# A pre-LN attention and GEGLU block: VectorE's exponential in one product of 2048 columns, 84 of 512 quads on VectorE, 12 slots turned there, and a new order

## The chip, the core and the metric

One Trainium2 chip, one of its cores, one launch. The metric is the device time of the kernel in microseconds (us); smaller is better. Beside the times there is one execution recorded by the hardware profiler. Engines are called as the profile calls them: PE is the matmul engine and PEld its weight load, ACT is ScalarE, DVE is VectorE, POOL is GpSimd, and SP issues the DMAs.

## What is computed

The input `x` has 2048 rows of 640 bf16 numbers. With `ln` for a layer norm without gain and bias:

```
qkv = ln(x) @ wqkv                       # 32 heads of 20
p   = softmax(q @ k.T * 20**-0.5)        # per head, 2048 x 2048
h   = x + concat(p @ v) @ wo
out = h + (gelu_tanh(ln(h) @ w_gate) * (ln(h) @ w_up)) @ w_down     # 640 -> 1728 -> 640
```

The exponentials are 32 x 2048 x 2048 numbers, 134 million; on 128 partitions these are 2048 tiles of 128 x 512.

## The kernel before

**Tiles and quads.** Scores are made transposed: 128 keys on the partitions, queries in the columns. Heads go in groups of four (`g`, 8 of them), which use four row groups of PE. A tile is 128 x 512 scores of one head, and the four tiles of one group over the same keys are a quad: 512 quads in all. The queries are taken in chunks (`QR`): first 512 queries for the first six groups, then chunks of 256, and at the end four of 128. A chunk is cut into slots, 33 in all, most of them of 16 quads; slot 31 has 12 and slot 32 has 4.

**Two ways to an exponential.** Most tiles go through ACT: a unit of two or three PSUM banks is filled by score matmuls (`unit`, line 1154; matmuls, L1175) and read by one ACTIVATE of 1024 or 1536 columns. Two sets of banks alternate, (0,1,2) and (3,4), so that PE fills one while ACT reads the other; in the slots of `FOUR` they are (0,1) and (2,3), so every instruction there has 1024 columns. The tiles of `D_QUADS[slot]` quads go to DVE instead (`d_exp`, line 1104). For each of the four tiles, a TENSOR_SCALAR of 512 columns (L1116) takes the scores out of PSUM as int16 numbers whose high bits are the exponent and whose low seven are the fraction. After the fourth, 2048 columns are worked at once: one TENSOR_SCALAR cuts out the fraction (`y`), a TENSOR_TENSOR multiplies it by the raw value, in `D_SPLIT` pieces (lines 1123 to 1126), and a second TENSOR_SCALAR reduces the raw value to its power of two (`v`). Both `y` and `v` are multiplied with the values by PE, so that each quad on DVE costs PE twice the attention-times-values work. These helpers record all instructions as L560.

**Where a DVE tile's scores lie.** In a slot of `DIN`, a DVE tile that falls due at a unit of three banks takes the third bank of that set; ACT then reads only two. This is called an inset here. The bank comes free when DVE has taken the tile out. In the other slots, and in all slots of `FOUR`, the tile has a background bank (7, 5 or 4) of its own. `D_LEAD` says by how many ACT tiles a DVE tile is placed ahead.

**Epilogue of a slot** (`epilogue`, line 1266). The sum of a slot collects in bank 6. For the chunks in `TURN`, DVE turns it by a 32 x 32 transpose, divides, turns it back, and four DMAs per slot write it to HBM, from where one DMA per chunk gathers it. For other chunks DVE copies it out, PE transposes it in four fp32 blocks (L1302), and DVE divides; from the third chunk on SP then issues a DMA transpose for each 128 rows.

**Background.** The projections of later groups and chunks, the output projection, layer norm and MLP of finished chunks (L866, L1417, L1537, their evacuations on DVE, tanh on ACT) run between all this.

**Order.** Nothing is ordered by the hardware. `Sched` lists some 6,700 operations with a cost and a priority and plans a start for each; every engine's program is the order that comes out. `NUDGE` adds to the sort key of single operations, and `HOLD` keeps an operation back until another has been started. An engine executes in that order, and waits on semaphores where the operation at its head isn't ready. The first 29 us are a prologue (load `x`, layer norm, transposes, keys and queries of the first group). The end is a tail: output projection, layer norm, MLP of the last 128 rows after the last exponential.

Of the kernel before, what the change touches and what calls it, by code (L numbers as in the profile page):

```python
# [47 lines left out]
class Sched:  # L48
# [325 lines left out]
FOUR = (24, 25)  # L374
DIN = (6, 14, 17, 18, 20, 23, 24, 27, 29, 30, 31, 32)
# [22 lines left out]
TURN = (3, 4, 6, 7, 8)  # L398
# [8 lines left out]
D_SPLIT = 2  # L407
D_LAG = 2
D_QUADS = (0, 0, 3, 2, 3, 3, 3, 3, 3, 2, 3, 3, 3, 1, 3, 3, 4, 2, 4, 3, 3, 3, 4, 3, 3, 3, 2, 2, 4, 3, 1, 2, 1)
D_FIRST, D_PART = 2, 0.8  # L410
D_LEAD = ((0, 0, 0, 0, 0, 0, 0, 0), (0, 21, 15, 8, 38, 7, 13, 18, 19, 16, 22, 21, 14, 33, 19, 19, 14, 7, 8, 10, 20, 0, 27, 25, 15))
# [127 lines left out]
def bass_sequential_preLN__mha_block__glu_gated_geglu__prompt_kernel(  # L539
# [12 lines left out]
    with ExitStack() as es:  # L552
# [709 lines left out]
        def epilogue(s_, bk, d_sums):  # L1262
# [7 lines left out]
            tb = rbase(c)  # L1270
            if c in TURN:
                n = len(gs)
# [378 lines left out]
```

## Time and profile before

| | us |
|---|---|
| runs | 854.5, 855.43, 855.63 |
| median | 855.43 |
| profiled execution | 855.09 |
| its span, first to last instruction | 853.3 |

In the profile, a group of instructions has a line, an engine, an operation, what it writes and reads, and a count; behind these come its busy time, the mean duration of one, and the idle time of the engine just before them with what ended it. Durations of ACT and DVE overlap a little: the next instruction starts before the last one's recorded end. What one instruction costs in a row of them is therefore read from the chain of work or from starts, not from the mean.

### The profile page before, as it was taken

The page shows a single profiled execution, that of the slowest core. Times are in us where ns is not written, and L with a number is a line of the kernel's source. Part 1 is how long each engine was busy: PE and PEld are TensorE (multiplying, and loading weights), DVE is VectorE, ACT ScalarE, POOL GpSimd, SP SyncE. Part 2 cuts the span into 40 slices and gives each one's busy share as a digit, 9 for nine tenths or more (in the row PEclk, how much of TensorE's full clock was granted, in tenths as well). Part 3 has the DMA queues.
Part 4 walks back from the last instruction along what each step waited for, and adds up shares of the span by engine and source line. Part 5 has one row for each costly group of instructions (what it writes and reads, how often), then busy time and mean ns, then how long its engine had stood idle before and what let it go on. Part 6 is the DMA issues. An engine that isn't in the chain of part 4 may idle for free.

```text
span 853.3 us, 31794 instructions
## 1 busy us (share of the span) xinstructions
PE 810.5 (95%) x14355; PEld 418.2 (49%) x14381; DVE 736.1 (86%) x1451; ACT 828.8 (97%) x824; POOL 65.2 (8%) x194
## 2 busy tenths in 40 slices
PE   8999999999999999999989999998999999999998
PEld 4433232233345554554444445444455666667677
DVE  8735888989989989978999899989998898897884
ACT  7999999999999999999999999999999999999992
POOL 6600000000101000100001000010002020020100
PEclk9999999999999999999999999999999999999999
DMA  8211113632431001001000100011001110101000
GB/s 277 83 34 52 44 36 78 166 84 69 133 95 20 7 14 32 18 19 36 7 21 2 26 25 2 18 28 30 7 22 14 45 21 16 38 4 27 11 12 17
DMA packets 41943, 36.07 MB, mean 42 GB/s; under 512 B 17524, under 2 KB 39968, under 8 KB 41808
## 3 DMA queue, kind: packets, MB, share of 16 engines
q1 hardware_dynamic: 41808, 34.04, 15.0%
q8 instruction: 113, 1.85, 1.0%
q14 instruction: 22, 0.18, 0.1%
HBM read 21.51 MB, written 9.40 MB: 36 GB/s over the span
## 4 chain that ended last, share of the span: by engine, by line
ACT 84%; PE 10%; DVE 3%; DMA 1%; POOL 1%; issue 1%; SPq 0%
ACT pts L560 55%; ACT rege L560 27%; ACT qt_all L560 3%; PE ps L1175 2%; PE ps L1537 2%; PE ps L560 2%; PE ps L1417 1%; PE ps L866 1%; DMA rege<-in_A_x_dram 1%; DVE qt_all L1116 1%; DVE rege L1116 0%; DVE rege L560 0%; PE ps L800 0%; DVE stats L560 0%; PE ps L861 0%
## 5 line engine op out<-in xcount | busy, mean ns | idle before, releaser
L560 ACT ACTIVATE pts<-ps 128x1536 bf16<-128x1536 f32 (+1 forms) x483 | 553.0, 1321 | 0.5 <-PE ps L1175 0.4
L1175 PE MATMUL ps<-qt_all,kt_all 32*128 32x256 bf16 (+2 forms) x4736 | 317.8, 257 | 25.9 <-ACT pts L560 8.2
L560 ACT ACTIVATE rege<-ps 128x1536 bf16<-128x1536 f32 (+1 forms) x235 | 281.8, 1319 | 0.6 <-PE ps L1175 0.5
L1175 PEld LDWEIGHTS ps<-qt_all,kt_all 32*128 32x128 bf16 x4736 | 118.9, 92 | 217.7 <-ACT pts L560 91.8
L1116 DVE TENSOR_SCALAR qt_all<-ps 128x512 int16<-128x512 f32 x176 | 118.7, 681 | 15.3 <-PE ps L1175 14.4
L1417 PE MATMUL ps<-rege,regw 128*128 128x256 bf16 (+1 forms) x1128 | 128.2, 250 | 1.5 <-DVE qt_all L1116 0.8
L1116 DVE TENSOR_SCALAR rege<-ps 128x512 int16<-128x512 f32 x160 | 108.1, 683 | 15.1 <-PE ps L1175 14.5
L560 PE MATMUL ps<-pts,v_all 128*21 128x256 bf16 (+2 forms) x2648 | 118.5, 260 | 0.7 <-ACT pts L560 0.6
L1417 PEld LDWEIGHTS ps<-rege,regw 128*128 128x128 bf16 x1128 | 81.1, 98 | 35.9 <-issue 18.2
L560 PE MATMUL ps<-rege,v_all 128*21 128x256 bf16 (+2 forms) x1676 | 97.0, 267 | 0.4 <-DVE rege L560 0.2
L866 PE MATMUL ps<-regw 128*128 128x512 bf16 (+1 forms) x283 | 67.8, 343 | 3.3 <-issue 1.7
L1537 PE MATMUL ps<-regw,rege 128*128 128x320 bf16 x378 | 69.7, 302 | 0.6 <-DVE rege L1376 0.3
L560 PEld LDWEIGHTS ps<-pts,v_all 128*21 128x21 bf16 x2648 | 57.2, 91 | 26.2 <-issue 18.2
L560 DVE TENSOR_SCALAR qt_all<-qt_all 128x2048 int16<-128x2048 int16 (+3 forms) x118 | 58.0, 496 | 0.9
L560 PEld LDWEIGHTS ps<-rege,v_all 128*21 128x21 bf16 x1676 | 41.4, 91 | 23.9 <-issue 16.8
L560 POOL CAST mv<-mv 128x4 bf16<-128x4 f32 (+2 forms) x13 | 3.6, 274 | 543.3 <-DVE mv L560 543.2
L1537 PEld LDWEIGHTS ps<-regw,rege 128*128 128x128 bf16 x378 | 30.1, 97 | 24.0 <-issue 9.7
L1462 DVE TENSOR_SCALAR rege<-ps 128x512 bf16<-128x512 f32 (+2 forms) x54 | 35.1, 653 | 5.7 <-PE ps L1417 4.8
L866 PEld LDWEIGHTS ps<-regw 128*128 128x128 bf16 x303 | 23.6, 97 | 32.4 <-issue 16.9
L1476 DVE SCALAR_TENSOR_TENSOR qt_all<-qt_all,ps 128x512 bf16<-128x512 f16 (+2 forms) x54 | 35.0, 649 | 4.3 <-PE ps L1417 2.8
L560 ACT ACTIVATE qt_all<-qt_all 128x512 f16<-128x512 f16 (+2 forms) x54 | 38.3, 739 | 0.0
L560 DVE TENSOR_SCALAR rege<-rege 128x2048 int16<-128x2048 int16 x54 | 37.0, 685 | 0.7
(150 smaller groups left out, 826.7 us busy)
## 6 DMA issues: line engine op xcount, KB each, us to landing
q_rows<-regw SPq DMA_DIRECT2D x20, 128.0 KB, 1.8
out_dram<-rege SPq DMA_DIRECT2D x16, 160.0 KB, 1.8
regw<-in_A_wqkv_dram SPq DMA_DIRECT2D x3, 800.0 KB, 11.1
rege<-in_A_x_dram SPq DMA_DIRECT2D x7, 320.0 KB, 4.0
regw<-in_B_w_gate_dram SPq DMA_DIRECT2D x5, 432.0 KB, 3.4
regw<-in_B_w_up_dram SPq DMA_DIRECT2D x5, 432.0 KB, 3.3
rege<-in_A_x_dram SPq DMA_DIRECT2D x3, 640.0 KB, 7.0
kt_all<-k_rows SPq DMA_DIRECT2D x12, 160.0 KB
```

Source lines behind the costliest of these rows:

```text
L560: return lambda eng: getattr(eng, method)(*args, **kwargs)
L866: yield op("pe", lambda eng, l=l, r=r, k=k: eng.matmul(bank(bk, n), l, r, start=(k == 0), stop=(k == len(steps) - 1), skip_group_check=Tru ...
L1116: d_ops.append(op("dve", lambda eng: eng.tensor_scalar(v[:, 512 * h:512 * h + 512], bank(b), EXP_MUL, 0.0, ALU.mult, ALU.max), c_dve(512), ...
L1175: return lambda eng: eng.matmul(out()[:, kk * nq:(kk + 1) * nq], kt_all[32 * j:32 * j + 32, g, kt * 128:(kt + 1) * 128], qt_all[32 * j:32 ...
L1417: op("pe", lambda eng, a=a, f=f, fi=fi: eng.matmul(bank(bk)[:, fi * nq:(fi + 1) * nq], w[:, a, F0[f]:F0[f] + 128], hnT[:, a, 128 * tb:128 ...
L1462: op("dve", lambda eng, bg=bg, fv=hv(k, w), w=w: eng.tensor_scalar(fv, bank(bg, w), 0.5, None, ALU.mult), c_dve(w), p, reads=[kg], writes= ...
L1476: op("dve", lambda eng, bu=bu, z=z, w=w: eng.scalar_tensor_tensor(out=z, in0=z.bitcast(F16), scalar=1.0, in1=bank(bu, w), op0=ALU.add, op1 ...
L1537: op("pe", lambda eng, f=f, o=o, wt=wt, bk=bk: eng.matmul(bank(bk, 320), ha_f[:, o:o + 128], wt, start=(f == 0), stop=(f == NF - 1), skip_ ...
```

## The change

Five constants of the plan, and the order:

```diff
-FOUR = (24, 25)
-DIN = (6, 14, 17, 18, 20, 23, 24, 27, 29, 30, 31, 32)
+FOUR = (22, 24, 25)
+DIN = (6, 14, 17, 20, 22, 23, 24, 28, 29, 30, 32)
...
-TURN = (3, 4, 6, 7, 8)
+TURN = (3, 4, 7, 8)
...
-D_SPLIT = 2
+D_SPLIT = 1
...
-D_QUADS = (0, 0, 3, 2, 3, 3, 3, 3, 3, 2, 3, 3, 3, 1, 3, 3, 4, 2, 4, 3, 3, 3, 4, 3, 3, 3, 2, 2, 4, 3, 1, 2, 1)
+D_QUADS = (0, 0, 3, 2, 3, 3, 3, 3, 3, 3, 3, 2, 3, 1, 3, 3, 4, 2, 4, 3, 3, 3, 4, 3, 3, 3, 2, 1, 5, 2, 1, 2, 1)
...
-D_LEAD = ((0, 0, 0, 0, 0, 0, 0, 0), (0, 21, 15, 8, 38, 7, 13, 18, 19, 16, 22, 21, 14, 33, 19, 19, 14, 7, 8, 10, 20, 0, 27, 25, 15))
+D_LEAD = ((0, 0, 0, 0, 0, 0, 0, 0), (0, 27, 20, 4, 38, 7, 13, 19, 18, 16, 22, 22, 14, 32, 20, 19, 14, 11, 10, 10, 17, 0, 33, 23, 26))
```

`D_QUADS` adds up to 85 before and 84 after. `TURN` loses chunk 6 (slots 20 to 23), so that 12 slots are turned on DVE instead of 16. All entries of `NUDGE` and `HOLD` are replaced. Before, the first numbers in them are 297 and 354, so that the prologue's first operations stand in the plain order of their priorities; after, `NUDGE` begins at 263 and `HOLD` like this, with entries for operations of the prologue:

```
HOLD = {
    3: 4, 44: 45, 57: 95, 60: 77, 90: 80, 106: 115, 107: 117, 128: 288, 168: 292, 197: 209, 226: 132, 238: 202, 283: 431, 317: 335, 320: 246, 322:
    427, 327: 428, 362: 525, 390: 382, 406: 545, 410: 342, ...
```

195 rows, old and new, of tables (HOLD, NUDGE) are left out of this document.

## The prediction

> **What bounds the kernel now.** I read the page first: its span, the busy shares, and the chain that ended last.
>
> ```profile
> span 853.3 us, 31794 instructions
> PE 810.5 (95%) x14355; PEld 418.2 (49%) x14381; DVE 736.1 (86%) x1451; ACT 828.8 (97%) x824; POOL 65.2 (8%) x194
> ...
> ACT 84%; PE 10%; DVE 3%; DMA 1%; POOL 1%; issue 1%; SPq 0%
> ```
>
> ACT is busy for 97% and holds 84% of the chain. An average hides stages, so I next took the window from the first exponential to the last tanh ahead of the tail; columns are length, then busy time and count of PE, PEld, DVE, ACT, POOL, then the granted clock.
>
> ```profile
> 29.65:831.86 802.21, 766.09 (x13942) 388.85 (x13964) 701.69 (x1358) 801.49 (x772) 47.47 (x146) 1.00 0.14 36
> ```
>
> ACT is busy 801.49 of 802.21 us. DVE is free for 100 us of this window. So 94% of the span lasts as long as ACT's list of work, and the remaining 29.65 + 21.4 us are the prologue and the tail. What ACT's list consists of, by form:
>
> ```profile
> L560 ACT ACTIVATE pts<-ps 128x1024 bf16<-128x1024 f32 x298 | 325.5, 1157 | 0.1
> L560 ACT ACTIVATE pts<-ps 128x1536 bf16<-128x1536 f32 x184 | 292.4, 1589 | 0.4 <-PE ps L1175 0.4
> ...
> L560 ACT ACTIVATE rege<-ps 128x1024 bf16<-128x1024 f32 x146 | 161.3, 1155 | 0.5 <-PE ps L1175 0.5
> L560 ACT ACTIVATE rege<-ps 128x1536 bf16<-128x1536 f32 x89 | 141.2, 1586 | 0.1
> L560 ACT ACTIVATE qt_all<-qt_all 128x512 f16<-128x512 f16 x45 | 33.3, 768 | 0.0
> ...
> L560 ACT ACTIVATE pts<-ps 128x512 bf16<-128x512 f32 x1 | 0.7, 667 | 0.0
> ```
>
> 444 instructions of two tiles, 273 of three and one of one make 1708 tiles: the 2048 of the problem less 4 x 85 on DVE. Their recorded means overlap, so the cost of one comes from the chain of waits, where pieces don't overlap:
>
> ```profile
> 34.27 2.26 ACT rege L560 x2
> ...
> 641.74 5.50 ACT pts L560 x6
> ...
> 819.57 0.51 ACT qt_all L560
> ```
>
> The first is one instruction of 1536 and one of 1024 columns, 2.26 us for five tiles. The second stands in a slot of two-bank units: 5.50 / 6 = 0.917 us for 1024 columns. So 1536 take 1.343, a further tile is worth 0.427, and the fixed part of an instruction is 0.917 - 2 x 0.427 = 0.063 us. Check: 273 x 1.343 + 444 x 0.917 + 0.5 + 45 tanh of 0.51 + about 3 for nine smaller tanh = 800.3 of 802.2. Some 1.9 us in 802 are late starts, all that another order could win in this window.
>
> **The change part by part.** *One quad fewer on DVE.* ACT gets four tiles: 4 x 0.427 = 1.71 us. This lies on the path; nothing hides it.
>
> *Number of ACT instructions.* With sets of three and two banks, five tiles take two instructions; in `FOUR`, four tiles do. Each inset takes a third tile from ACT's instruction, which makes 0.4 instructions more. Before: slots 24 and 25 have 104 ACT tiles, 52 instructions; the other 1604 tiles need 641.6; 718 are there, so 24.4 come from insets, 61 of them. Eleven slots can have insets (24 stands in `DIN` too, but has no third bank), with 27 quads, 108 tiles: 56% of them are inset. After: slot 22 joins `FOUR` with 48 tiles, and nine slots with 23 quads, 92 tiles, can have insets, some 52. Instructions: 152 / 2 + 1560 / 2.5 + 52 x 0.4 = 720.8, or 2.8 more, 0.18 us. `D_LEAD` moves tiles between neighbouring slots; I allow six instructions either way, 0.4 us. The sum on ACT is 1.9 us.
>
> [...]
>
> *The product in one piece.* Two instructions of 1024 columns become one of 2048.
>
> ```profile
> 563.76 1.28 DVE L560 TENSOR_TENSOR dwx<-qt_all,dwx 128x1024 bf16<-128x1024 bf16 x2
> ...
> L560 DVE TENSOR_TENSOR dwx<-qt_all,dwx 128x1024 bf16<-128x1024 bf16 x48 | 32.0, 681 | 0.2
> ...
> L560 DVE TENSOR_TENSOR rege<-rege,qt_all 128x512 bf16<-128x512 bf16 x45 | 18.5, 414 | 0.2
> ```
>
> Two in a row span 1.28 and the second lasts 0.68, so one start follows the other by 0.60. Halving the columns saves 681 - 414 = 267 ns, so 2048 should hold DVE for 0.60 + 2 x 0.267 = 1.13 us instead of 1.20. Saved: 0.07 x 84 = 6 us of DVE. The dropped quad saves 4 evacuations and 4 instructions of about 0.60, 4.8 us. DVE is not on the path, so both count nothing directly; the cover is its 100 free us. What can be felt is latency: whatever stands behind the product in DVE's order waits up to 1.13 instead of 0.60 us.
>
> *Four slots no longer turned (chunk 6).* DVE loses one transpose per slot, PE gains four fp32 transposes, and SP exchanges 17 DMAs (four per slot and one gather) for two DMA transposes.
>
> ```profile
> L560 DVE STREAM_TRANSPOSE osb<-ox 128x512 bf16<-128x512 bf16 x16 | 11.2, 703 | 0.0
> ...
> L1302 PE MATMUL ps<-identf,osb 128*128 128x128 f32 x64 | 13.0, 293 | 0.8 <-DVE rege L1542 0.4 <-DVE v_all L1013 0.2
> ...
> 767.36 1.22 SPq L560 DMA_TRANSPOSE rege<-ox  x1
> ...
> 29.33 0.45 SPq L560 DMA_DIRECT2D q_rows<-regw  x1
> ```
>
> That is 4 x 0.62 = 2.5 us less on DVE (0.70 recorded, less the 0.08 of overlap seen above), and 16 x 13.0 / 64 = 3.3 us more on PE, placed in background time. On SP, two transposes at 1.22, 2.4 us, replace 17 issues at about 0.45, 7.7 us; who waits for them is the output projection of that chunk, background work with a slot's length to spare. On the path: nothing. If PE's cover were gone, at most 3.3 us.
>
> *The order.* Within the window it can win the 1.9 us of late starts or lose more. In the prologue this is what stands ahead of the first exponential:
>
> ```profile
> 26.20 0.69 DVE L902 TENSOR_REDUCE kd<-ps 128x1 f32<-128x512 f32 x1
> ...
> 27.07 0.59 ACT L909 ACTIVATE regw<-ps 128x512 bf16<-128x512 f32 x1
> ...
> 27.91 0.75 DVE L997 TENSOR_SCALAR qt_all<-ps,off 128x512 bf16<-128x512 f32 x1 [0.22 <-PE ps L993]
> ...
> 28.26 0.69 ACT L930 ACTIVATE kt_all<-ps,one 128x512 bf16<-128x512 f32 x1 [0.26 <-PE ps L925]
> ...
> 29.21 0.60 PE L1175 MATMUL ps<-qt_all,kt_all 32*128 32x512 bf16 x5
> ...
> 29.65 2.36 ACT L560 ACTIVATE pts<-ps 128x1536 bf16<-128x1536 f32 x2 [0.37 <-PE ps L1175]
> ```
>
> The queries are ready at 28.66, but the scores start at 29.21, behind the key's evacuation by ACT (L930, to 28.95), which empties a bank. An order that frees that bank sooner wins up to 0.55 us; a worse one loses as much. Operations further up (transposes and projections held behind each other) may give another 1 us either way. I take 0, since the rows show no side. The tail's steps are the same; I allow 0.5 us either way.
>
> The sum: 855.09 for the profiled execution + 1.9 = 857.0. Its distance to the median of 855.43 is 0.34, within the spread of the runs (854.5 to 855.63). A measurement of this kernel can tell 0.2% from no change, 1.7 us: under 853.7 is faster, over 857.1 slower. The forecast stands almost on the upper bound.
>
> **The rivals.** *The late starts vanish.* DVE gives back 6 + 4.8 + 2.5 = 13 us, and scores that wait for it start in time. For it: the stall quoted below ends on DVE. Against: nothing shows that the new order doesn't make others. All 1.9 us won: 855.1, the same as now.
>
> *Faster.* The same, and the prologue gives 0.55 at its end and 1 further up: 857.0 - 1.9 - 1.55 = 853.5, just past the bound. For it: `HOLD` and `NUDGE` now reach into the prologue, which nothing had touched. Against: everything has to come together, because 1.9 us of ACT's own work must first be paid.
>
> *Slower: the evacuation of an inset stands behind a whole product.* An inset's bank is freed by DVE, and the scores of the whole next unit in that set wait for it. The trace has such a case:
>
> ```profile
> 766.29 0.68 DVE L1116 TENSOR_SCALAR qt_all<-ps 128x512 int16<-128x512 f32 x1
> ...
> 767.12 0.40 PE L1175 MATMUL ps<-qt_all,kt_all 32*128 32x128 bf16 x12 [1.14 <-DVE qt_all L1116]
> ...
> 767.56 1.02 ACT L560 ACTIVATE rege<-ps 128x1024 bf16<-128x1024 f32 x1 [0.34 <-PE ps L1175]
> ```
>
> DVE took the tile out late, the scores waited 1.14 us, ACT lay idle 0.34. An unsplit product in front adds up to 0.53 us to such a delay. There are 23 quads in slots with insets, one product each; if nine of them meet an evacuation at 0.34 us, that is 3 us: 860. It decides once the 1.7 us of the bound are passed, at five. For it: slot 28 gets five quads and becomes a `DIN` slot. Against: an order made for the long product can put evacuations ahead, and there are fewer insets, 52 for 61.
>
> *The change doesn't do what it says.* If the product at 2048 columns took as long as two of 1024, DVE would have 6 us more and the time would be the forecast's. Only at half its pace (84 x 1.1 us, most of DVE's free 100) would DVE hold up ACT, and the time would pass 860; the steady cost from 512 to 1024 columns speaks against it.
>
> **How the numbers follow.** The forecast, 855.9 to 858.3 around 857.0 with the allowances above: 0.48, of which 0.27 lies within 0.2% and 0.21 above. Late starts vanish, 855.1: 0.16, the same. Faster, 853.5: 0.14. Insets behind products, 860: 0.20. Product at half pace: 0.02. So faster 0.14, the same 0.43, slower 0.43. The range from 853.8 to 860.0 leaves out the far parts of the two outer cases, some 0.2.
>
> **What would show it.** Right: ACT instructions of two and three tiles with 1712 tiles in all, about 721 of them; the window from first to last exponential 1.9 us longer, ACT without gaps; the product as 84 instructions of 128x2048 at about 1.2 us recorded; the first exponential at 29.65 give or take 0.6. Wrong: a window that is shorter than before (late starts were dearer than I count), a first exponential before 28.5 (the prologue was the point), or idle time of ACT that ends on scores which waited for L1116.

## The result and the profile after

The changed kernel takes 860.69 us (median of 5 runs, 860.1 to 864.84) against 855.38 us before (5 runs): a ratio of 1.0076, 95% interval 1.0051 to 1.0101. It is slower by 5.3 us, and the forecast of 857.0 and its upper end of 860.0 both lie under it. The profiled execution took 860.1 us. Line numbers are 20 lower than before: L540 is the helper, L1155 the scores, L1096 the evacuation of a VectorE tile, L1522 the addition that takes an MLP output out of PSUM.

The page, the same lines as before:

```profile
span 858.4 us, 32100 instructions
PE 817.7 (95%) x14571; PEld 420.7 (49%) x14571; DVE 723.1 (84%) x1355; ACT 830.8 (97%) x823; POOL 63.8 (7%) x194
...
ACT 74%; PE 14%; DVE 9%; DMA 1%; POOL 1%; issue 1%; SPq 0%
```

ACT is still busy for 97%, but its share of the chain fell from 84% to 74%; PE went from 10% to 14% and DVE from 3% to 9%. The busy shares hardly show this, the chain does. The stretch from the first exponential to the end of the last one, by the windows view (same columns as before):

```profile
29.95:836.57 806.62, 773.08 (x14138) 391.29 (x14137) 689.13 (x1263) 803.62 (x772) 46.11 (x146) 1.00 0.14 35
```

In the kernel before, the last exponential ended at 831.55, so this stretch was 801.9 us; it is 4.7 longer. ACT lies visibly idle for 3.0 us of it, against 0.7 of the 802.2 before. ACT's exponentials by form:

```profile
L540 ACT ACTIVATE pts<-ps 128x1024 bf16<-128x1024 f32 x295 | 323.1, 1157 | 1.8 <-PE ps L1155 1.7
L540 ACT ACTIVATE pts<-ps 128x1536 bf16<-128x1536 f32 x187 | 297.9, 1593 | 0.6 <-PE ps L1155 0.5
L540 ACT ACTIVATE rege<-ps 128x1024 bf16<-128x1024 f32 x144 | 160.6, 1154 | 0.0
L540 ACT ACTIVATE rege<-ps 128x1536 bf16<-128x1536 f32 x91 | 145.5, 1599 | 0.9 <-PE ps L1155 0.9
```

There are 439 instructions of two tiles and 278 of three, 1712 tiles. By the prices of the prediction they take 439 x 0.917 + 278 x 1.343 = 775.9 us, against 774.3 before: 1.65 us more work. The last column is the other part: the idle time that ended on scores went from 1.1 us (0.1 + 0.4 + 0.5 + 0.1) to 3.3.

A wait hides partly behind the overlap of ACT's instructions (1.157 us recorded for 1024 columns on the mean, 0.904 from start to start), so I also counted from starts: of every ACT instruction between the first and the last exponential, the time to the next start less the shortest such time for its form (0.904 us for 1024 columns, 1.331 for 1536), summed where it is over 0.1 us. This **late-start sum** is 5.0 us in the profiled run before and 7.9 in the one after. The account: 1.65 of work, 2.9 of late starts and 0.3 of a later first exponential (29.95 for 29.65) make 4.85 of the 5.0 us by which the profiled executions differ.

Where ACT starts late in the kernel after, in its timeline (start, duration, instruction, and in brackets the visible idle time and who ended it; three pieces of the run):

```profile
570.32 1.72 ACT L540 ACTIVATE pts<-ps 128x1536 bf16<-128x1536 f32 x1
572.68 1.02 ACT L540 ACTIVATE pts<-ps 128x1024 bf16<-128x1024 f32 x1 [0.64 <-PE ps L1155]
573.90 1.45 ACT L540 ACTIVATE pts<-ps 128x1536 bf16<-128x1536 f32 x1 [0.20 <-PE ps L1155]
...
667.68 1.02 ACT L540 ACTIVATE pts<-ps 128x1024 bf16<-128x1024 f32 x1 [0.44 <-PE ps L1155]
...
676.73 1.14 ACT L540 ACTIVATE rege<-ps 128x1024 bf16<-128x1024 f32 x1
678.37 1.45 ACT L540 ACTIVATE rege<-ps 128x1536 bf16<-128x1536 f32 x1 [0.50 <-PE ps L1155]
```

Counted by starts, 572.68 is 1.03 us late, 573.90 0.32, 667.68 0.73 and 678.37 0.74; 580.46, of the same kind as 678.37, is 0.70 late. What the scores had waited for, in PE's timeline:

```profile
572.25 0.39 PE L1155 MATMUL ps<-qt_all,kt_all 32*128 32x256 bf16 x6 [0.72 <-DVE rege L1522]
...
666.90 0.41 PE L540 MATMUL ps<-dwx,v_all 128*21 128x128 bf16 x16 [0.69 <-DVE dwx L540]
...
677.92 0.62 PE L1155 MATMUL ps<-qt_all,kt_all 32*128 32x128 bf16 x20 [0.52 <-ACT rege L540]
```

Three waits, of two kinds. At 677.92 the scores wait for ACT itself. Slot 25, a slot of `FOUR`, ends with a unit in banks (2,3) that ACT reads until 677.87 (676.73 + 1.14), and the next slot begins with a unit in (0,1,2), which needs bank 2. At 580.46 the same happens where slot 22, new in `FOUR`, begins. At 666.90 PE waits for a product of 2048 columns. That product is late itself: the chain of work that ends at 667.68 runs through a chain of small operations on POOL, for whose result DVE stands still 0.92 us before 663.53 (start, duration, what):

```profile
663.30 0.20 POOL sd L540
...
663.53 0.17 DVE rs L540
...
665.63 1.24 DVE dwx L540
...
666.90 0.41 PE ps L540 x16
...
667.68 1.02 ACT pts L540
```

At 572.25 the origin is of this second kind too, in DVE's timeline:

```profile
567.37 1.22 DVE L540 TENSOR_TENSOR dvx<-rege,dvx 128x2048 bf16<-128x2048 bf16 x1
570.32 0.17 DVE L540 RECIPROCAL rs<-sd 128x2 f32<-128x2 bf16 x1 [1.74 <-POOL sd L540]
570.40 0.67 DVE L540 TENSOR_SCALAR rege<-rege 128x2048 int16<-128x2048 int16 x1
570.99 0.80 DVE L540 TENSOR_SCALAR ox<-rege,mu,rs 128x640 bf16<-128x640 bf16 x2
571.71 0.48 DVE L1522 TENSOR_TENSOR rege<-ps,rege 128x320 bf16<-128x320 f32 x1
572.11 1.30 DVE L1096 TENSOR_SCALAR qt_all<-ps 128x512 int16<-128x512 f32 x2
```

DVE's next instruction is the reciprocal of a layer norm's root, which POOL computes in such a chain. DVE stands still for 1.74 us, and the evacuations queued behind it, which free banks for scores, come late. Over the whole kernel DVE's waits for these roots are no longer than they were; they are two instead of four, and other work stands behind them. Before, then after (total us, times, longest):

```profile
DVE rs L560 <- POOL sd L560: 2.8, 4, 1.2
```

```profile
DVE rs L540 <- POOL sd L540: 2.7, 2, 1.7
```

### The profile page after: what moved, and what is told of

Same layout as the page of the kernel before. It is cut to its first block, busy times and chain, and to the rows that moved or that the text cites. A ratio compares the mean times of both kernels' runs of the same rounds, so it can differ in the third digit from the quotient of the medians.

```text
span 858.4 us, 32100 instructions
## 1 busy us (share of the span) xinstructions
PE 817.7 (95%) x14571; PEld 420.7 (49%) x14571; DVE 723.1 (84%) x1355; ACT 830.8 (97%) x823; POOL 63.8 (7%) x194
## 4 chain that ended last, share of the span: by engine, by line
ACT 74%; PE 14%; DVE 9%; DMA 1%; POOL 1%; issue 1%; SPq 0%
ACT pts L540 48%; ACT rege L540 23%; PE ps L1155 3%; PE ps L1397 3%; DVE qt_all L1096 2%; ACT qt_all L540 2%; PE ps L540 2%; PE ps L846 2%; PE ps L1517 1%; DVE qt_all L540 1%; DMA regw<-in_A_wqkv_dram 1%; PE ps L841 1%; DVE rege L1096 1%; DVE dwx L540 1%; DVE dvx L540 1%
## 5 line engine op out<-in xcount | busy, mean ns | idle before, releaser
L540 ACT ACTIVATE pts<-ps 128x1536 bf16<-128x1536 f32 (+1 forms) x482 | 555.7, 1326 | 2.3 <-PE ps L1155 2.1
L1155 PE MATMUL ps<-qt_all,kt_all 32*128 32x256 bf16 (+2 forms) x4736 | 312.7, 258 | 25.2 <-ACT pts L540 10.1
L540 ACT ACTIVATE rege<-ps 128x1536 bf16<-128x1536 f32 (+1 forms) x235 | 285.1, 1326 | 0.9 <-PE ps L1155 0.9
L1155 PEld LDWEIGHTS ps<-qt_all,kt_all 32*128 32x128 bf16 x4736 | 117.6, 92 | 217.4 <-ACT pts L540 87.6
L1397 PE MATMUL ps<-rege,regw 128*128 128x256 bf16 (+1 forms) x1108 | 126.4, 250 | 1.8 <-DVE qt_all L1096 1.1
L1096 DVE TENSOR_SCALAR qt_all<-ps 128x512 int16<-128x512 f32 x172 | 115.6, 685 | 14.7 <-PE ps L1155 13.7
L1096 DVE TENSOR_SCALAR rege<-ps 128x512 int16<-128x512 f32 x160 | 108.1, 685 | 15.6 <-PE ps L1155 14.7
L540 PE MATMUL ps<-pts,v_all 128*21 128x256 bf16 (+2 forms) x2658 | 120.2, 260 | 0.1
L540 PE MATMUL ps<-rege,v_all 128*21 128x256 bf16 (+2 forms) x1682 | 97.7, 267 | 0.6 <-DVE rege L540 0.6
L1397 PEld LDWEIGHTS ps<-rege,regw 128*128 128x128 bf16 x1108 | 78.4, 98 | 37.1 <-issue 20.4
L846 PE MATMUL ps<-regw 128*128 128x320 bf16 (+1 forms) x305 | 71.4, 345 | 1.8 <-DVE rs L540 1.0
L540 PEld LDWEIGHTS ps<-pts,v_all 128*21 128x21 bf16 x2658 | 58.4, 92 | 27.4 <-issue 20.3
L1517 PE MATMUL ps<-regw,rege 128*128 128x320 bf16 x354 | 64.3, 302 | 0.7 <-DVE rege L1522 0.3
L540 DVE TENSOR_SCALAR qt_all<-qt_all 128x2048 int16<-128x2048 int16 (+3 forms) x116 | 56.8, 497 | 0.7
L540 PEld LDWEIGHTS ps<-rege,v_all 128*21 128x21 bf16 x1682 | 42.0, 91 | 23.3 <-issue 14.5
L540 POOL CAST mv<-mv 128x4 bf16<-128x4 f32 (+2 forms) x13 | 2.9, 219 | 547.1 <-DVE mv L540 546.9
L540 ACT ACTIVATE qt_all<-qt_all 128x512 f16<-128x512 f16 (+2 forms) x54 | 39.3, 748 | 0.0
L841 PE MATMUL ps<-rege,regw 128*32 128x256 bf16 (+1 forms) x928 | 37.5, 262 | 0.7 <-issue 0.7
```

The costliest lines, as they stand in the source:

```text
L540: return lambda eng: getattr(eng, method)(*args, **kwargs)
L841: return [lambda eng, j=j: eng.matmul(PS[32 * j:32 * j + 32, 512 * bk.b + lo:512 * bk.b + hi], l[:, 32 * j:32 * j + 32], r, start=start, s ...
L846: yield op("pe", lambda eng, l=l, r=r, k=k: eng.matmul(bank(bk, n), l, r, start=(k == 0), stop=(k == len(steps) - 1), skip_group_check=Tru ...
L1096: d_ops.append(op("dve", lambda eng: eng.tensor_scalar(v[:, 512 * h:512 * h + 512], bank(b), EXP_MUL, 0.0, ALU.mult, ALU.max), c_dve(512), ...
L1155: return lambda eng: eng.matmul(out()[:, kk * nq:(kk + 1) * nq], kt_all[32 * j:32 * j + 32, g, kt * 128:(kt + 1) * 128], qt_all[32 * j:32 ...
L1397: op("pe", lambda eng, a=a, f=f, fi=fi: eng.matmul(bank(bk)[:, fi * nq:(fi + 1) * nq], w[:, a, F0[f]:F0[f] + 128], hnT[:, a, 128 * tb:128 ...
```

## The experiments

Two explanations stood against each other for the 2.9 us. **The long instruction**: a product of 2048 columns holds DVE for 1.13 us at a time, and POOL's chain with it. **The order**: what stands ahead of what, once two halves are one operation that can't have anything between them, and the places where the new order puts urgent work. Twelve kernels were run; each ratio is to runs of the kernel before on the same chip, whose medians lie between 854.99 and 855.75 us. The late-start sum is that of the profiled run. In exp_repeat, merged, merged_late, apart_in_two, halves and exit_bank PE's granted clock fell in that run (to a mean of 0.994 to 0.998; counted at half, that is about 3.4 to 10.3 us), which is part of their sums; in the other rows it did not.

| kernel | median us | ratio to before, 95% | profiled run us | late-start sum us |
|---|---|---|---|---|
| before | 855.0 to 855.8 | | 855.09 | 5.0 |
| after | 860.69 | 1.0051 to 1.0101 | 860.10 | 7.9 |
| exp_repeat | 859.29 | 1.0030 to 1.0058 | 859.15 | 5.5 |
| merged | 861.43 | 1.0047 to 1.0081 | 863.41 | 13.4 |
| merged_late | 860.99 | 1.0044 to 1.0080 | 860.41 | 9.8 |
| pairs_adjacent | 854.96 | 0.9987 to 1.0006 | 854.22 | 4.7 |
| pairs_apart | 862.25 | 1.0066 to 1.0096 | 861.80 | 11.2 |
| apart_in_two | 864.41 | 1.0087 to 1.0121 | 864.88 | 14.6 |
| halves | 862.83 | 1.0071 to 1.0098 | 863.92 | 11.4 |
| exit_bank | 861.91 | 1.0052 to 1.0097 | 864.38 | 11.8 |
| both_banks | 861.93 | 1.0058 to 1.0089 | 861.56 | 8.3 |
| root_later | 859.54 | 1.0033 to 1.0067 | 859.28 | 6.7 |
| halves_root | 860.53 | 1.0043 to 1.0073 | 860.33 | 6.3 |
| exit_root | 858.32 | 1.0024 to 1.0054 | 858.17 | 5.3 |

**Is ACT's work worth its list price?** The kernel before, with eight more exponentials of one tile each, written to an unused buffer.

```diff
+AGAIN = (150, 203, 300, 353, 450, 503, 600, 653)
+            if len(exp_ops) in AGAIN:
+                sc.again.append((exp_ops[-1], I("activation", scr[:, 0:512], PS[:, 512 * s0:512 * s0 + 512], ACT.Exp, ...)))
```

> The kernel before, order kept, with eight ACT instructions more, at eight units spread over the middle: each computes 512 columns of exponentials that are also computed by the unit itself, into columns that nothing reads. Price of tiles on ACT: if ACT's list alone sets the length there, 8 x 0.49 = 3.9 us more, 859.3. If ACT had slack between late starts, part of it is absorbed: under 858. If PE or DVE set the pace, no change.

859.29 against 855.35: 3.94 us for eight, where 8 x (0.063 + 0.427) gives 3.9. The interval is 2.6 to 5.0 us, so the price is confirmed to about a third, and the 1.65 us of ACT's longer list count in full or nearly so.

**The product in one piece, all else as before.** All 85 products of the kernel before as one instruction, at the place that the earlier half had in DVE's order; then the same at the place of the later half.

```diff
+        gone = {b: a for a, b in self.pairs}
+        order = [o for o in order if o.i not in gone]
...
+        for a, (_, fn) in zip((x for x, _ in self.pairs), self.full):
+            ops[a].fns = [fn]
```

> The kernel before, every engine's order kept, only the two product instructions of each of the 85 quads made one of 2048 columns, at the place of the first. If ACT's list, the bank sets and the order make the difference (theory A), the product alone changes nothing: 855.4, give or take 0.5. If the long product does it by keeping POOL from its operands (theory B), POOL instructions of over 1 us appear beside the product, DVE waits longer for the layer norm's root, and the time rises by 0.5 to 2 us: 856 to 857.5. If evacuations of insets behind the product are dear (the prediction's slower rival, C), ACT starts late behind L1116 in the inset slots: 858 or more.

> As the run merged (the kernel before, order kept, the product in one piece), but the product of 2048 columns stands at the place of the later of its two halves, so that whatever stood between the halves on DVE now stands ahead of it. If the long product costs by what it keeps waiting behind it on DVE (theory C, with the clock's loss that follows when PE waits), the time goes back to the kernel before's: 855.4, give or take 0.7, clock 1.0. If it costs by holding POOL off (theory B), it stays dear, since POOL is held as long as in merged: 857 or more.

861.43 and 860.99: in the order made for halves, the long product costs 6.1 and 5.9 us, at either place. Theories A and B named too little for merged, and C was wrong for merged_late; no theory held in both. Neither run says whether the instruction or the displaced order is to blame; the late place doesn't restore the old order either. A likely reason, not tested: the earlier half had filled time in which DVE otherwise waits for scores (DVE's idle time at its evacuations, by the page's two groups of them, is 30.4 us before and 35.7 in merged_late).

**The two explanations taken apart.** In DVE's order of the kernel before, 39 of the 85 pairs of halves are neighbours; in 46, something stands between. First the 39 alone were merged, then the 46 alone, and last the 46 were drawn together at the earlier place but left as two instructions.

```diff
+        at = {o.i: n for n, o in enumerate(o for o in order if o.eng == "dve")}
+        both = [(p, f) for p, f in zip(self.pairs, self.full) if abs(at[p[1]] - at[p[0]]) == 1]
```

(`!= 1` in pairs_apart; in apart_in_two `ops[a].fns = ops[a].fns + ops[b].fns` in place of the one full product.)

> The kernel before with only those 39 of its 85 products in one instruction of 2048 columns whose halves already stand next to each other in VectorE's order; nothing else moves. Theory of the order (the piece hurts because its second half is pulled ahead of evacuations that stood between): 855.3, no change. Rival, the hold of GpSimd (a 2048-column product holds the layer norm's operations 1.0 to 1.2 us instead of at most 0.66, and VectorE's reciprocal root waits): 39/85 of the merged kernel's loss of about 5.5 us, so some 857.5 to 858.

> The kernel before with the other 46 products in one instruction, at the place of the earlier half, and the 39 neighbouring pairs left in two. Theory of the order: the whole loss of the merged kernel, 860.5 to 861.5. Rival, the hold of GpSimd: 46/85 of it, 858 to 858.5.

> The kernel before with the order of VectorE that the run of the 46 separated products had (the later half pulled up to its partner), but every product still two instructions of 1024 columns; the two of a pair signal once, after the second. If the moved order is the cost and the instruction's size is not: again 861.5 to 863, or a little more for the two start-ups. If the one long instruction is the cost: back to 855 to 856.5.

854.96, 862.25 and 864.41. Merging 39 neighbours changes nothing; merging the other 46 costs all that merging 85 costs, 6.5 us; and drawing those 46 together without merging them costs more still, 9.4 us. In the kernel before, then, the cost is the displaced order and not the long instruction: with the same displacement that is, if anything, the cheaper form. Nor is it that both halves are now signalled together, since the 39 neighbours are too. And it needs no loss of clock, which was 1.000 in the profiled run of pairs_apart. How the displacement works, in DVE's timeline before, and then with the pair merged:

```profile
295.63 0.68 DVE L560 TENSOR_TENSOR dwx<-qt_all,dwx 128x1024 bf16<-128x1024 bf16 x1
296.24 0.68 DVE L1116 TENSOR_SCALAR rege<-ps 128x512 int16<-128x512 f32 x1
296.84 0.68 DVE L1476 SCALAR_TENSOR_TENSOR qt_all<-qt_all,ps 128x512 bf16<-128x512 f16 x1
297.43 0.68 DVE L1116 TENSOR_SCALAR rege<-ps 128x512 int16<-128x512 f32 x1
298.03 0.68 DVE L560 TENSOR_TENSOR dwx<-qt_all,dwx 128x1024 bf16<-128x1024 bf16 x1
```

```profile
296.65 1.22 DVE L570 TENSOR_TENSOR dwx<-qt_all,dwx 128x2048 bf16<-128x2048 bf16 x1
297.78 0.68 DVE L1126 TENSOR_SCALAR rege<-ps 128x512 int16<-128x512 f32 x1
```

Before, the evacuation started 0.61 us after the product's first half; now it starts 1.13 after the product. PE and then ACT behind it in pairs_apart:

```profile
298.52 0.39 PE L1187 MATMUL ps<-qt_all,kt_all 32*128 32x256 bf16 x2 [0.56 <-DVE rege L1126]
```

```profile
300.16 2.37 ACT L570 ACTIVATE rege<-ps 128x1536 bf16<-128x1536 f32 x2 [0.39 <-PE ps L1187]
```

Over the whole kernel it is in the group of the 256-column scores, whose last column names who ended PE's idle time. The kernel before:

```profile
L1175 PE MATMUL ps<-qt_all,kt_all 32*128 32x256 bf16 x2304 | 178.5, 272 | 16.5 <-ACT pts L560 5.6 <-ACT rege L560 2.8 <-DVE qt_all L1116 1.8
```

The 39 neighbours merged (pairs_adjacent):

```profile
L1187 PE MATMUL ps<-qt_all,kt_all 32*128 32x256 bf16 x2304 | 178.7, 272 | 16.8 <-ACT pts L570 5.9 <-ACT rege L570 3.5 <-DVE qt_all L1126 1.5
```

The other 46 merged (pairs_apart):

```profile
L1187 PE MATMUL ps<-qt_all,kt_all 32*128 32x256 bf16 x2304 | 178.1, 272 | 20.9 <-ACT pts L570 4.6 <-DVE qt_all L1126 3.9 <-DVE rege L1126 3.8
```

These 46 drawn together, in two instructions (apart_in_two):

```profile
L1187 PE MATMUL ps<-qt_all,kt_all 32*128 32x256 bf16 x2304 | 178.2, 273 | 21.5 <-DVE qt_all L1126 4.4 <-ACT pts L570 3.9 <-DVE rege L1126 3.8
```

PE waiting for ACT is the healthy case: ACT is busy and PE ahead of it. Waits for the evacuations on DVE, the harmful case, grow from 1.8 and 0.5 (too small to be named in the line) to 7.7 and 8.2 us in all where the pairs were drawn together. In the kernel after, whose order was made for the long product, they are 3.1:

```profile
L1155 PE MATMUL ps<-qt_all,kt_all 32*128 32x256 bf16 x2304 | 175.7, 273 | 17.2 <-ACT pts L540 7.4 <-DVE qt_all L1096 1.6 <-DVE rege L1096 1.5
```

**The same question in the new order.** The kernel after, with each product as two instructions of 1024 in succession.

```diff
-            for m in range(0, 4, 4 // D_SPLIT):
...
+            d([I("tensor_tensor", y[:, z].bitcast(BF16), v[:, z].bitcast(BF16), y[:, z].bitcast(BF16), ALU.mult)
+               for z in (slice(0, 1024), slice(1024, 2048))], 1.06, vk + yk, yk)
```

> The changed kernel, every engine's order kept, each product issued again as two instructions of 1024 columns in direct succession. A: no change, 860.7. B: POOL is kept waiting for at most 0.7 us at a time instead of 1.2, the layer norm's chain at 564 to 570 us ends about 1 us sooner, the late starts of ACT at 572 to 574 and at 668 us, 2.1 us together, shrink below 1: about 859.2. C: no change, since an evacuation still stands behind both halves.

862.83, no faster than after, and over all three forecasts. The late start at 572 shrinks from 1.03 to 0.75 us, since POOL's chain is held less (its longest operation near by is 0.66 instead of 1.19 us), but it stays, and in the profiled run the clock fell right behind it. So the long instruction has a part of some 0.3 us in this one wait. The run's time can't price it, since the clock was below 1.000 in all five runs; halves_root and root_later, below, differ by the same edit with a full clock in both profiled runs, and there two short instructions save 0.4 us of late starts (6.3 for 6.7) and no time (860.53 for 859.54).

**The root's place.** The kernel after, with DVE's reciprocal at 570 us, another at 664 us, and the scalings that use them, moved behind four other instructions of DVE, so that they come fifth.

```diff
+ROOTS, LATER = (8, 10), 4
+            r = [o for o in dve if o.tag == ("rs", t)][-1]
+            group = [r] + [o for o in dve if r.i in o.deps]
...
+            n = rest.index(next(o for o in dve[dve.index(r):] if o not in group)) + LATER
+            dve = rest[:n] + group + rest[n:]
```

> The changed kernel, order kept, except that on DVE the reciprocal of the layer norm's root and its two applications stand five instructions later, for the fifth and sixth chunk (570 and 664 us), where DVE waited for POOL. If that wait is what makes ACT late at 572 to 574 us (1.35 us) and what lets PE idle until its clock drops in some runs: late starts there under 0.4, 859.3, clock 1.0 in every run. If the bank sets and the list alone matter: 860.7 as before, and drops of the clock go on.

859.54, 1.15 us under after, as the late-start sum says (7.9 to 6.7). The intervals of the two against before overlap, so it is the trace that shows the gain: the late starts at 572.68, 573.90 and 667.68, 2.1 us together, are gone, while the one at the first border of `FOUR` grows from 0.70 to 0.91 and smaller ones come. POOL's chain is held just as long here, beside the same products (POOL's timeline in root_later; the last row is the same operation with no product beside it):

```profile
565.46 1.19 POOL L555 TENSOR_SCALAR rs<-nw 128x2 int32<-128x2 int32 x1
...
567.95 1.04 POOL L555 TENSOR_SCALAR nw<-nw 128x2 f32<-128x2 f32 x1
...
570.36 0.19 POOL L555 TENSOR_SCALAR nw<-nw 128x2 f32<-128x2 f32 x1
```

yet ACT runs through 572 us, because the evacuations now stand ahead of the root in DVE's order, and DVE no longer waits for POOL at all. It was the place of the wait in DVE's order, not the length of POOL's chain, that cost time.

**The borders of `FOUR`.** The kernel after with the last unit of slot 25 in banks (3,4), so that the next slot's (0,1,2) is free (exit_bank); then both borders mended so, with a new local order from 570 to 690 us (both_banks); then the border of slot 25 together with the later roots (exit_root).

```diff
+        for u in range(1, len(units) - 1):
+            if units[u][0][0] in FOUR and ubank[u] == 2 and any(units[w][0][0] not in FOUR and ubank[w] == 0 for w in (u + 1,)):
+                ubank[u] = 3
```

> The changed kernel, with the last two-bank unit of slot 25 in banks (3,4) instead of (2,3), so that the next unit's banks (0,1,2) are not the ones that ACT is reading. A: the late start of 0.74 us at 678 us goes, the one of 0.70 at 580 stays: 860.0. B and C: no change at 678 us, since nothing of DVE or POOL was touched: 860.7.

> The changed kernel with (3,4) instead of (2,3) for the first two-bank unit behind a unit in (0,1,2) and for the last one ahead of such a unit; some holds and nudges of operations between 570 and 690 us are replaced so that the plan has no late start of ACT above 0.25 us left there. If overlapping bank sets cost what the trace shows (0.70 and 0.74 us at 580 and 678 us): 859.3, both late starts gone. If something else takes their place: 860 or more. The rest of the loss stays in any case: 1.65 us of ACT's list and 0.3 us ahead of the first exponential.

> The changed kernel with the roots later and the last two-bank unit of slot 25 on banks 3 and 4. If stalls add up (late start of 0.73 us at 678 us gone for good): 859.5 less 0.7, 858.8. If a stall that is taken away there is only put off to the next full set of banks, as it was with the banks alone: 859.5 to 860.

861.91, 861.93 and 858.32. Alone, the mended border shows no gain: its runs at a granted clock of 1.000 took 859.73 and 860.62, the others, at 0.994 and 0.996, 864.38 and 863.19. In its trace the border's late start is gone, but 0.49 and 0.46 us come behind it (units begun at 681.54 and 684.58). Both borders with a new local order are no better: their own late starts are gone, but the stall at 572 is still there (1.03), a new one of 0.58 comes at 749, and four of its five runs have a clock of 0.996, so its time settles nothing about the borders. With the root's wait gone, the border's 0.74 us do come off: 858.32 after 859.54 (the intervals overlap here too), and a late-start sum of 5.3 after 6.7. Exit_root is the best of the changed orders, and its late starts are nearly those of the kernel before (5.0). What is left, 2.6 us of medians, is nearly all of it ACT's 1.65, 0.5 of its later first exponential (30.17) and 0.3 of late starts.

**The clock behind the wait.** Halves and root_later together.

> The kernel of two halves in succession with the two reciprocal roots at 570 and 664 us, and what they scale, five instructions later on VectorE. Theory (the wait for the root starves TensorE at 572 us, and that is what halves the clock from 575 to 585 us): both the late starts of 0.75 and 0.3 us and the clock's fall go, 862.8 becomes 859.5 or less, at a clock of 1.000. Rival (the clock falls for another reason): only the late starts go, 861.8, and the clock stays near 0.996.

860.53, with the clock at 1.000 in three runs of four and 0.998 in the fourth; halves had 0.994 to 0.998. Windows of 3.5 us in halves, and the same in halves_root (length, then PE, PEld, DVE, ACT, POOL, the granted clock):

```profile
571.50:575.00 3.50, 2.27 (x38) 0.87 (x34) 2.70 (x6) 2.87 (x3) 0.00 (x0) 0.98 0.48 94
575.00:578.50 3.50, 3.50 (x35) 0.93 (x23) 2.20 (x4) 2.71 (x3) 0.00 (x0) 0.50 0.00 0
578.50:582.00 3.50, 3.46 (x29) 1.40 (x30) 2.16 (x5) 2.26 (x3) 0.00 (x0) 0.50 0.11 36
582.00:585.50 3.50, 3.50 (x55) 1.60 (x48) 1.98 (x4) 2.25 (x3) 0.00 (x0) 0.55 0.05 18
```

```profile
571.50:575.00 3.50, 2.89 (x43) 1.22 (x43) 2.75 (x6) 3.50 (x5) 0.00 (x0) 1.00 0.24 47
575.00:578.50 3.50, 2.98 (x43) 1.39 (x41) 3.43 (x7) 3.50 (x4) 0.00 (x0) 1.00 0.28 58
```

With the wait, PE is busy 2.27 of 3.5 us, and then the clock is at half for some 10 us, in which ACT loses about 3.3 us (2.71, 2.26 and 2.25 of 3.5). Without the wait PE is busy 2.89, and the clock stays. The late-start sum falls from 11.4 to 6.3. The expected 859.5 wasn't reached: in the profiled run the exponentials end as early as that (835.23), but the way out of the last output behind DVE's last instruction is 1.5 us longer than in after (854.77 to 858.6 instead of 856.08 to 858.4); the cause of that is open.

In the kernel after the clock is a matter of chance: its five runs have clocks of 1.000 (three, 860.1 to 860.69) and of 0.996 and 0.994 (862.6 and 864.84). Only a run at 1.000 has a trace, so that the other two lost it at this wait is likely and not shown. In the 14 runs of root_later, halves_root and exit_root the clock is never under 0.998.

## Why the prediction was wrong

*ACT's work.* Right within 0.3: 1712 tiles as said, 717 instructions where I said 720.8, so 1.65 us instead of 1.9, and exp_repeat agrees with the price.

*The product.* Right: 84 instructions with a mean of 1.217 to 1.220 us recorded in their four large groups, and the next starts 1.13 after it (296.65 to 297.78 in pairs_apart). That it would stand off the path was right for the instruction, as pairs_adjacent shows.

*The order: the step that failed.* "Within the window it can win the 1.9 us of late starts or lose more", and the forecast took nothing for it. Measured: 2.9 us lost. Two things were wrong there. The 1.9 was a remainder, a sum of 772 instructions at prices read from the chain, taken from 802. The chain's 0.917 us is itself above the commonest step of 0.904, so part of the late starts sat in the price; the direct count from starts gives 5.0 in the same profile, so the order was worth more, both ways, than I allowed. And I took DVE's idle time as a whole for the cover ("the cover is its 100 free us"), where the cover that counts is local: at 568 to 570 us DVE was itself standing still, with urgent work queued behind.

*The late starts.* What took the time was none of the steps I priced. The largest places in after are the waits for POOL at two roots (1.03 and 0.32 us behind the first, 0.73 behind the second; moving both brought 1.15 net) and two borders of `FOUR` (0.70 and 0.74; the second came off in exit_root, the first only together with a new local order). The borders could have been read from the code. Laid out, the plan before has two borders of `FOUR`, and the bank sets on both sides share bank 2 at one of them, where ACT runs a tanh in between (625.81 us); the plan after has four borders, shares bank 2 at two, and has nothing in between.

*The slower rival* named 860 and an evacuation behind an unsplit product. The time came out about right by luck. The mechanism exists, and pairs_apart shows it; but in after the large late starts are of other kinds, since its order was made for the long product. So its time was met by other causes.

*Prologue and tail.* The first exponential is 0.3 later, inside the 0.55 allowed. From the end of the last exponential to the end it is 21.8 us in both.

*Insets.* I expected 52 after 61; with 717 instructions in place of 720.8 there are some nine fewer than that, by the same arithmetic (3.8 / 0.4); the kernels' plans, laid out, have 60 before and 43 after. That too makes the rival's condition harder to meet.

Still open: a late start of 0.67 us at 723, where PE itself stands still for reasons that the trace doesn't name; what the turned slots and the moved quads did to the order, which no run took alone; why the first exponential starts 0.3 us later; and whether an order exists for 84 quads that is better than before. At exit_root's late starts, ACT's longer list alone keeps it 1.65 us behind.

## What to carry to other kernels

Two neighbouring instructions on an engine that isn't the bound could become one here for nothing (39 pairs, 854.96 us); where something stood between them, merging is a reordering, and is priced as one. Count the late starts of the bound engine from start to start before saying what an order can win or lose, and give the order a term of its own with a losing side. On an engine that works in order (in after DVE stood still for 1.74 us with evacuations queued behind its wait), ask what is queued behind each wait for a slow chain: moving the wait behind four instructions gained more here than shortening it.

## What the runs showed of the hardware

**GpSimd's small operations lasted longer beside a long instruction of VectorE.** They take 0.19 us while VectorE stands still (569.55 in after), but 1.19 and 1.04 beside a product of 2048 columns (565.46 and 567.95 in root_later), and at most 0.74 beside one of 1024 in the kernel before (560.50). So one small operation lasted nearly as long as the whole product, 1.22 us. The product is not the only such instruction. In the kernel before, the longest of these operations stands beside a TENSOR_SCALAR of 2048 columns (695.39, 0.71 us):

```profile
695.37 0.77 POOL L560 TENSOR_SCALAR sd<-mv 128x1 bf16<-128x1 bf16 x1
```

In pairs_adjacent one lasted 1.14 us beside a product (695.86, 1.21 us), and ACT behind it was not late:

```profile
695.99 1.14 POOL L570 TENSOR_TENSOR nw<-rs 128x1 f32<-128x1 f32 x1
```

**TensorE's granted clock fell to half for stretches of some 3 to 10 us.** In windows of 3.5 us of the profiled runs it was down to 0.50 in halves, exit_bank and merged, and to 0.53 in merged_late. Counted at half, that is about 10.3 us in halves and exit_bank (575 to 585), 6.8 in merged (511 to 518) and 3.4 in merged_late (771 to 774). Merged has a further fall between 200 and 300 us (a mean of 0.98 there). Exp_repeat and apart_in_two have a mean of 0.998 over the run, at half about 3.4 us. A fall and the return in merged_late (columns as above):

```profile
767.50:771.00 3.50, 2.35 (x79) 1.75 (x78) 2.56 (x7) 3.34 (x4) 1.20 (x5) 0.98 0.02 5
771.00:774.50 3.50, 3.17 (x66) 1.94 (x66) 2.37 (x5) 2.05 (x2) 0.00 (x0) 0.53 0.24 47
774.50:778.00 3.50, 3.37 (x78) 1.92 (x78) 2.93 (x5) 3.11 (x3) 0.00 (x0) 1.00 0.02 5
```

In halves, exit_bank and merged_late the clock fell after 3.5 us with PE busy 2.27, 2.19 and 2.35 of them, 63 to 67%; in after, the same 2.27 left it at 1.00, and so did 2.11 of 3.41 us in the kernel before (764.79 to 768.20). So the busy share doesn't say by itself when the clock falls, and no run here shows what does. Nor does it say when the clock comes back: in merged_late it was at 1.00 after one window with PE busy 3.17 of 3.5, while in halves it took three, with PE busy 3.46 of 3.5 or more.
